# RWKV-6 attention and a tanh-shrink MLP in one kernel: unused matmuls in the boot's waits, and the result in two parts

## The chip, the cores and the metric

The kernel runs on one core of a Trainium2 chip. The metric is the device time of one execution in microseconds (us). Its engines work in parallel, each through its own instructions in order, and wait for each other by semaphores: TensorE (PE in the profile; its weight loads are PEld), VectorE (DVE), ScalarE (ACT), GpSimd (POOL) and SyncE (SP), which issues most DMA transfers.

## The reference, cut to what matters

```python
batch, n_heads, seq, head_dim = (4, 8, 768, 48)
for t in range(S):
    cur = np.einsum('bhd,bhe->bhde', u[None] * kt, vt)
    y[:, :, t] = np.einsum('bhd,bhde->bhe', rt, state + cur)
    state = wt[:, :, :, None] * state + np.einsum('bhd,bhe->bhde', kt, vt)
# y -> x: (3072, 384)
h = x @ w_in            # 384 x 2048
g = h - np.tanh(h)
return g @ w_out        # 2048 x 384, float32
```

A recurrence over 768 steps for each of 32 heads, then a two-layer MLP on the 3072 rows that come out.

## The kernel before

The sequence is cut into 8 blocks of 384 steps (4 batches, 2 halves each). Attention of a block is made in phases: "level 1" to "level 32" build the matrix of scores between time steps inside chunks of 64 by doubling (at level m the keys and receptances of blocks of m steps are multiplied, and then decayed for the next level), "turn" transposes the keys, "update" makes the chunks' states, and "result" adds what comes from the states to what comes from the scores. While the MLP of block i runs, the phases of block i+1 are threaded between its products. Only the first block has nothing to run beside: its attention is the "boot". There the four pairs of heads are worked in two halves, h1 and h2, so that engines overlap.

A level in the boot: products on TensorE into a PSUM scratch tile (2 banks of 512 columns, of which a level uses 192 in each, and level 1 uses 384), decay on VectorE, then masked copies into the scores.

```python
def scratch(ps):
    return ps.tile([P, 2, BANK], F32, name="att", tag="att")     # 4 buffers in the boot

def level(self, ps, m, p0, n, put_off=None):
    ...                                       # cut: level 32 puts its copies off
    gr = self.gram(ps, self.tiles["kq"], self.tiles["rp"], p0, n, m, L // 2)   # TensorE, 24 products
    ins = self.decay(m, p0, n)                # VectorE: kq and rp times the decay
    if 2 * m % 32 == 0:
        ...                                   # cut: level 16 copies on ScalarE, 4 copies
        return ins
    for h in range(2):
        ...
        nc.vector.copy_predicated(out=dst, mask=mask, data=src)    # reads gr
    return ins
```

The result, all pairs of a block or half of them:

```python
def result(self, ps, pairs, holes_full=False):
    yp = [scratch(ps) for e in range(2)]
    ...
                nc.tensor.matmul(yp[p % 2][e0:e0 + 64, par, n0:n0 + L],     # from the states
                                 lhsT=St[rows, p, 2 * c + par, :], rhs=rp[rows, t0:t0 + L],
                                 start=(n == 0 and c == 0), stop=False, skip_group_check=True)
    nc.tensor.drain().then_inc(fence, 1)
    fences.append(None)
    nc.tensor.wait_ge(fence, len(fences))
    ...
                nc.tensor.matmul(yp[p % 2][e0:e0 + D, par, n0:n0 + L],      # from the scores
                                 lhsT=self.v[toks, c, f0:f0 + D], rhs=A[toks, h, p, c, :],
                                 start=False, ...)
    ...                                       # ScalarE copies yp to xT; holes_full: 48 rows at a time
```

The boot and the main loop:

```python
def boot(ps, blk, later):
    h1, h2 = HALVES
    ...                                       # loads, mix
    masked = blk.level_1(ps, h1)              # products; the masked copy comes later
    blk.decay(1, h1, UP)
    blk.totals(1, h1, UP)
    blk.mix(h2, UP, copy=nc.scalar.copy)
    masked()
    blk.level(ps, 2, h1, UP)
    masked = blk.level_1(ps, h2)
    blk.decay(1, h2, UP)
    ...
    masked()
    for m in (2, 4, 8, 16, 32):
        for p0 in HALVES:
            if (m, p0) != (2, h1):
                ins = blk.level(ps, m, p0, UP, last)
            ...
    for p0 in HALVES:
        blk.turn(ps, p0)                      # transposes; ScalarE copies ks
    for copies in last:
        copies()                              # level 32's copies, ScalarE
    later.mix(0, NPAIR, ("kmix",))            # ScalarE
    for p0 in HALVES:
        blk.update(ps, p0)                    # products, then 24 VectorE instructions on the states
    blk.result(ps, [h1, h1 + 1])
    blk.fill_holes([nc.sync, nc.scalar, nc.gpsimd])
    converted()                               # weights made ready by ScalarE and VectorE
    ready.append(convert(*raws.pop(0)))
    converted()
    ins = blk.result(ps, [h2, h2 + 1], True)
    begin_behind(ins, more_weights(nc.sync))  # a weight load that starts with the result's first copy
    ...

for f in range(NF):                           # main loop, a block's 16 slices of the MLP
    g, next_rest, made = first(here, f, ps_d) # products hp, then ScalarE and VectorE
    ...
    if f in phases:
        later.phase(ps_a, phases[f])
    ...
    if len(waiting) > LAG:
        s, fs, gs = waiting.pop(0)
        s.add(fs, gs)                         # products acc of slice f - 3
```

Of the kernel before, what the change touches and what calls it, by code (L numbers as in the profile page):

```python
# [37 lines left out]
F32 = mybir.dt.float32  # L38
# [46 lines left out]
def kernel(  # L85
# [26 lines left out]
    u_sb = const.tile([P, NPAIR], F32, name="u_sb", tag="u_sb")  # L112
    nc.scalar.dma_start(out=u_sb, in_=uT)

    warm = const.tile([P, 1], F32, name="warm", tag="warm")
    nc.scalar.activation(out=warm, in_=shift[:, 0:1], func=AF.Copy)

# [57 lines left out]
            lambda: nc.vector.tensor_tensor(out=a, in0=a, in1=up, op=ALU.add)]  # L175


    def scratch(ps):
        return ps.tile([P, 2, BANK], F32, name="att", tag="att")

    fence, fences = tc.alloc_semaphore("fence"), []

    class Block:
# [189 lines left out]
                        in1=kvp[:, c % 2, n0:n0 + D], op0=ALU.mult, op1=ALU.add)  # L373
            return ins

        def result(self, ps, pairs, holes_full=False):


            St, rp = states[self.q], self.tiles["rp"]
            yp = [scratch(ps) for e in range(2)]  # L380
            slots = [pairs[n:n + 2] for n in range(0, len(pairs), 2)]
            for n, slot in enumerate(slots):
                for c in range(NCP):
                    for par in range(2):
                        for p in slot:
                            for h in range(2):
                                rows = slice(64 * h, 64 * h + D)
                                e0 = 64 * (h ^ (p % 2))
                                t0 = p * NB + (2 * c + par) * L
                                n0 = (n * NCP + c) * L  # L390
                                nc.tensor.matmul(yp[p % 2][e0:e0 + 64, par, n0:n0 + L],  # L391
                                                 lhsT=St[rows, p, 2 * c + par, :],
                                                 rhs=rp[rows, t0:t0 + L],
                                                 start=(n == 0 and c == 0), stop=False,
                                                 skip_group_check=True)

            nc.tensor.drain().then_inc(fence, 1)  # L397
            fences.append(None)
            nc.tensor.wait_ge(fence, len(fences))
            for n, slot in enumerate(slots):  # L400
                for p in slot:
                    for c in range(NCP):
                        for h in range(2):
                            for par in range(2):
                                toks = slice(64 * par, 64 * par + 64)
                                e0 = 64 * (h ^ (p % 2))
                                f0 = p * D2 + h * D
                                n0 = (n * NCP + c) * L
                                nc.tensor.matmul(yp[p % 2][e0:e0 + D, par, n0:n0 + L],  # L409
                                                 lhsT=self.v[toks, c, f0:f0 + D],  # L410
                                                 rhs=A[toks, h, p, c, :],
                                                 start=False,
                                                 stop=(n == len(slots) - 1 and c == NCP - 1),
                                                 skip_group_check=True)
            copies = []
            for n, slot in reversed(list(enumerate(slots))):
                for p in reversed(slot):
                    src = yp[p % 2][:, :, n * NCP * L:(n + 1) * NCP * L].rearrange(
                        "e a (c t) -> e c a t", t=L)
                    dst = self.xT[:, p, :] if p < KC else self.late  # L420
                    dst = dst.rearrange("e (c a t) -> e c a t", a=2, t=L)
                    for rows in (slice(0, D), slice(64, 64 + D)) if holes_full else (slice(0, P),):
                        copies.append(nc.scalar.copy(out=dst[rows], in_=src[rows]))  # L423
            return copies[0]

# [9 lines left out]
        def phase(self, ps, name):  # L435
            if name == "level 1":
                for p0 in HALVES:
                    self.level_1(ps, p0)()
            elif name == "turn":
                for p0 in HALVES:  # L440
                    self.turn(ps, p0)
            elif name == "update":
                for p0 in HALVES:
                    self.update(ps, p0)
            elif name == "result":
                self.result(ps, list(range(NPAIR)))
                self.fill_holes([nc.sync])
            else:
                self.level(ps, name, 0, NPAIR)
# [67 lines left out]

    def plan(i):

        names = ("level 1", 2, 4, 8, 16, 32, "turn", "update", "result")  # L520
# [12 lines left out]
        return dict(zip(steps, names)), before, behind, converted, loads, urgent  # L533
# [18 lines left out]
    def boot(ps, blk, later):  # L552

        h1, h2 = HALVES
        for p0 in HALVES:
            for name, src in (("kq", kT), ("rp", rT), ("wt", wT)):
                blk.load(name, src, p0, UP)
        for name in ("rmix", "kmix"):
            blk.tiles[name] = inp.tile([P, NPAIR * NB], F32, name=name, tag=name)
        more_weights(nc.sync)  # L560
        blk.load_v()
        for _ in range(2):
            more_weights(nc.sync)
        blk.mix(h1, UP, copy=nc.vector.tensor_copy)
        masked = blk.level_1(ps, h1)
        blk.decay(1, h1, UP)
        blk.totals(1, h1, UP)
        blk.mix(h2, UP, copy=nc.scalar.copy)
        masked()
        blk.level(ps, 2, h1, UP)  # L570
        masked = blk.level_1(ps, h2)
        blk.decay(1, h2, UP)
        blk.totals(1, h2, UP)
        for m in (2, 4, 8, 16):
            blk.totals(m, h1, UP)
# [64 lines left out]
    for i, blk in enumerate(blocks):  # L640
# [7 lines left out]
        for f in range(NF):  # L648
# [81 lines left out]
```

## Time and profile before

| | |
|---|---|
| median of 3 runs | 667.45 us (667.01 to 667.76) |
| span of the profiled execution | 665.8 us |
| TensorE busy | 642.6 us, 97% |
| VectorE busy | 545.2 us, 82% |
| ScalarE busy | 488.7 us, 73% |
| mean granted TensorE clock in the records | 0.990 |

The page lists for each engine how long it was busy and for groups of instructions their mean duration, and in 40 slices how busy each engine was. A slice is 16.6 us here, so the boot is the first three. The line for TensorE's granted clock shows full speed in every slice but the third, where it is 5 tenths. The trace can also be asked for the busy time in any stretch, for the instructions that write one tile (smallest, median and largest duration in ns), and for the instructions in order of time; a row of that list has start, duration, engine, line, operation, output and inputs, shape, and how many were merged, and in brackets how long the engine stood idle before and what ended it. One fp32 product shows as two TensorE passes, so 24 products are 48 passes.

The chain of waits, followed back from the last instruction, is TensorE for 80% of the span, VectorE 5%, ScalarE 4%, weight loads 4%.

### The profile page before, as it was taken

What the parts mean: (1) busy time and instruction counts of PE and PEld (TensorE: products, weight loads), DVE (VectorE), ACT (ScalarE), POOL (GpSimd) and SP (SyncE); (2) the same over time, 40 slices, a digit from 0 to 9 for tenths busy, and PEclk for the clock granted to TensorE, in tenths of its full rate; (3) what the DMA queues carried; (4) which work ended last, traced back from release to release, by engine and by line L of the source; (5) the groups of instructions that cost most, each with busy time, mean ns of one, the idle gap of its engine ahead of it and who ended that gap; (6) DMA issues with size and microseconds to landing.
All of it is one profiled execution on the core that took longest, in us unless ns stands there. A gap on an engine that the chain in (4) does not pass through costs nothing.

```text
span 665.8 us, 19964 instructions
## 1 busy us (share of the span) xinstructions
PE 642.6 (97%) x8480; PEld 412.0 (62%) x8480; DVE 545.2 (82%) x1101; ACT 488.7 (73%) x966; POOL 4.6 (1%) x19
## 2 busy tenths in 40 slices
PE   5879999999999999999999999999999999999997
PEld 4756656566665666666665666656666566655554
DVE  7789999899768997599885997689985999747664
ACT  4668998875868667785767758686677857768785
POOL 2000000000000000000000000000000000000000
PEclk9959999999999999999999999999999999999999
DMA  8656432532312122222212231123132200001000
GB/s 318 220 181 226 135 128 81 188 106 65 96 33 89 58 63 84 58 72 56 91 50 57 73 97 50 56 63 108 49 96 58 71 3 2 2 10 37 0 0 36
DMA packets 30841, 54.37 MB, mean 82 GB/s; under 512 B 2336, under 2 KB 28704, under 8 KB 30752
## 3 DMA queue, kind: packets, MB, share of 16 engines
q1 hardware_dynamic: 30336, 52.80, 24.5%
q8 instruction: 67, 1.10, 0.7%
q10 hardware_dynamic: 352, 0.25, 0.1%
q14 instruction: 22, 0.18, 0.1%
q0 software_dynamic: 64, 0.05, 0.0%
HBM read 47.19 MB, written 4.72 MB: 78 GB/s over the span
## 4 chain that ended last, share of the span: by engine, by line
PE 80%; DVE 5%; issue 4%; PEld 4%; ACT 4%; DMA 1%; PEldq 1%; SPq 0%; DVEq 0%
PE acc L509 33%; PE hp L471 32%; PE att L242 9%; PE att L409 2%; DVE states L371 2%; PEld hp L471 2%; PEld att L391 2%; PE att L342 2%; PEld acc L509 1%; PE att L319 1%; DMA wt<-in_wT 1%; DVE rp L274 1%; DVE w_sb L175 1%; ACT scores L330 1%; PEldq L397 1%
## 5 line engine op out<-in xcount | busy, mean ns | idle before, releaser
L471 PE MATMUL hp<-xT,w_sb 128*128 128x384 f32 x768 | 271.5, 490 | 3.8 <-ACT xT L423 2.1
L509 PE MATMUL acc<-w_sb,gT 128*128 128x384 f32 x768 | 273.6, 493 | 0.8 <-issue 0.8
L471 PEld LDWEIGHTS hp<-xT,w_sb 128*128 128x128 f32 x768 | 145.9, 191 | 108.0 <-ACT xT L423 2.3
L509 PEld LDWEIGHTS acc<-w_sb,gT 128*128 128x128 f32 x768 | 140.5, 190 | 89.5 <-ACT o L514 2.3
L478 ACT ACTIVATE h<-hp 128x384 f32<-128x384 f32 x128 | 62.6, 489 | 138.9 <-PE hp L471 138.1
L493 DVE TENSOR_TENSOR th<-h,th 128x384 f32<-128x384 f32 x128 | 71.0, 555 | 46.1 <-ACT th L482 46.0
L488 DVE SCALAR_TENSOR_TENSOR hs<-h,s 128x384 f32<-128x384 f32 x128 | 71.0, 555 | 26.3 <-ACT s L479 26.3
L496 DVE COPY_PREDICATED gT<-big,th 128x384 f32<-128x384 int32 x128 | 76.2, 595 | 12.8 <-ACT h L478 0.5
L480 ACT ACTIVATE qa<-s,shift 128x384 f32<-128x384 f32 x128 | 78.8, 615 | 4.2
L488 DVE SCALAR_TENSOR_TENSOR gT<-qb,hs 128x384 f32<-128x384 f32 x128 | 71.4, 558 | 9.3
L483 ACT ACTIVATE big<-s,shift 128x384 f32<-128x384 f32 x128 | 76.8, 600 | 0.0
L481 ACT ACTIVATE qb<-s,shift 128x384 f32<-128x384 f32 x128 | 76.8, 600 | 0.0
L488 DVE SCALAR_TENSOR_TENSOR hs<-qa,hs 128x384 f32<-128x384 f32 x128 | 70.6, 552 | 0.0
L479 ACT ACTIVATE s<-h 128x384 f32<-128x384 f32 x128 | 67.0, 524 | 4.0
L482 ACT ACTIVATE th<-h 128x384 f32<-128x384 f32 x128 | 64.9, 507 | 0.0
L242 PEld LDWEIGHTS att<-rp,kq 48*64 48x64 f32 x3072 | 53.4, 145 | 18.3 <-issue 12.6
L242 PE MATMUL att<-rp,kq 48*64 48x32 f32 x3072 | 57.5, 229 | 2.0 <-DVE rp L274 0.9
L274 DVE TENSOR_TENSOR kq<-kq,tot 128x768 f32<-128x768 f32 (+1 forms) x45 | 38.7, 859 | 2.9 <-PE att L242 1.5
L371 DVE SCALAR_TENSOR_TENSOR states<-states,tot,att 128x48 f32<-128x48 f32 x176 | 31.5, 259 | 9.1 <-PE att L360 9.1
L274 DVE TENSOR_TENSOR rp<-rp,tot 128x768 f32<-128x768 f32 (+1 forms) x45 | 38.8, 863 | 0.0
L302 DVE COPY_PREDICATED scores<-mask_all,att 128x384 f32<-128x384 uint8 (+1 forms) x54 | 31.9, 656 | 0.0
L242 PE MATMUL att<-rmix,kmix 48*64 48x64 f32 x768 | 15.3, 239 | 7.4 <-ACT rmix L222 7.4
(54 smaller groups left out, 339.4 us busy)
## 6 DMA issues: line engine op xcount, KB each, us to landing
raw<-in_weights SPq DMA_DIRECT2D x16, 768.0 KB, 4.9
rmix<-in_rT SPq DMA_DIRECT2D x7, 768.0 KB, 4.7
kmix<-in_kT SPq DMA_DIRECT2D x7, 768.0 KB, 4.8
wt<-in_wT SPq DMA_DIRECT2D x7, 768.0 KB, 4.8
kq<-in_kT SPq DMA_DIRECT2D x7, 768.0 KB, 5.7
rp<-in_rT SPq DMA_DIRECT2D x7, 768.0 KB, 4.6
v_sb<-in_v SPq DMA_DIRECT2D x8, 576.0 KB, 4.2
out_y<-o SPq DMA_DIRECT2D x23, 192.0 KB, 1.9
```

The costliest lines, as they stand in the source:

```text
L242: nc.tensor.matmul(dst, lhsT=lhs[rows, t0:t0 + L], rhs=src, start=True, stop=True)
L274: ins = nc.vector.tensor_tensor(out=part, in0=part, in1=by, op=ALU.mult)
L471: nc.tensor.matmul(hp, lhsT=w_in_sb[:, f, kc, :], rhs=xT[:, kc, :], start=(kc == KC - 1), stop=(kc == 0))
L479: nc.scalar.activation(out=s, in_=h, func=AF.Square)
L480: nc.scalar.activation(out=qa, in_=s, func=AF.Square, bias=shift[:, 0:1])
L481: nc.scalar.activation(out=qb, in_=s, func=AF.Square, bias=shift[:, 1:2])
L482: nc.scalar.activation(out=th, in_=h, func=AF.Tanh)
L483: nc.scalar.activation(out=big, in_=s, func=AF.Relu, bias=shift[:, 2:3])
L488: return lambda: nc.vector.scalar_tensor_tensor(out=out, in0=in0, scalar=scalar, in1=in1, op0=op0, op1=ALU.mult)
L493: lambda: nc.vector.tensor_tensor(out=th, in0=h, in1=th, op=ALU.subtract),
L496: lambda: nc.vector.copy_predicated(out=g, mask=big.bitcast(I32), data=th)], made
L509: nc.tensor.matmul(acc, lhsT=g[:, j * P:(j + 1) * P], rhs=w_out_sb[:, f, :], start=(f == 0), stop=(f == NF - 1))
```

## The change

It has three parts. (1) `result` becomes two functions, so that the products of an MLP slice stand between the products from the states and those from the scores; the wait for the fence is then meant to fall behind other work. (2) In the boot's first half, the products from the scores come first, as they are ready before the states; they leave the rows between heads untouched, so this half is copied 48 rows at a time too. (3) Unused fp32 products of a constant are put on TensorE where the boot leaves it waiting, to keep it busy[...]. They write columns of the last scratch tile that its phase doesn't use. Their results are read by nothing.

```diff
+    idle_in = const.tile([P, NB], F32, name="idle_in", tag="idle_in")
+    nc.vector.memset(idle_in, 1.0)
...
+    last_scratch = []
     def scratch(ps):
-        return ps.tile([P, 2, BANK], F32, name="att", tag="att")
+        last_scratch[:] = [ps.tile([P, 2, BANK], F32, name="att", tag="att")]
+        return last_scratch[0]
...
-        def result(self, ps, pairs, holes_full=False):
+        def from_states(self, yp, slots, first):      # the first loop of result; 48 columns wide if second
+        def from_scores(self, yp, slots, first):      # the second loop of result
+        def result_1(self, ps, pairs, part="from_states"):
+            yp = [scratch(ps) for e in range(2)]
+            slots = [pairs[n:n + 2] for n in range(0, len(pairs), 2)]
+            getattr(self, part)(yp, slots, True)
+            nc.tensor.drain().then_inc(fence, 1)
+            fences.append(None)
+            return yp, slots
+        def result_2(self, yp, slots, apart=False, part="from_scores"):
+            nc.tensor.wait_ge(fence, len(fences))
+            getattr(self, part)(yp, slots, False)
             ...                                       # the copies
...
     def boot(ps, blk, later):
         h1, h2 = HALVES
+        def keep_busy(n, width):
+            for _ in range(n):
+                nc.tensor.matmul(last_scratch[0][:, 0, BANK - width:], lhsT=idle_in[:, 0:P],
+                                 rhs=idle_in[:, 0:width], start=True, stop=True)
+        scratch(ps)
+        keep_busy(5, NB)
...
         masked = blk.level_1(ps, h1)
+        keep_busy(2, P)
...
         blk.level(ps, 2, h1, UP)
+        keep_busy(1, 320)
         masked = blk.level_1(ps, h2)
+        keep_busy(2, P)
...
                 if (m, p0) != (2, h1):
                     ins = blk.level(ps, m, p0, UP, last)
+                    keep_busy(1, 320)
...
-        blk.result(ps, [h1, h1 + 1])
+        blk.result_2(*blk.result_1(ps, [h1, h1 + 1], "from_scores"), True, "from_states")
...
-        ins = blk.result(ps, [h2, h2 + 1], True)
+        ins = blk.result_2(*blk.result_1(ps, [h2, h2 + 1]), True)
+        keep_busy(2, 320)
...
             if len(waiting) > LAG:
                 s, fs, gs = waiting.pop(0)
                 s.add(fs, gs)
+            if later and phases.get(f) == "result 1":
+                later.phase(ps_a, "result 2")
```

(Cut and condensed: the plan's names and the two loops' `start` and `stop` flags follow from this.)

More of the change, by code (lines that the diff above doesn't have):

```diff
@@ L374, in update @@
             return ins
-        def result(self, ps, pairs, holes_full=False):
-            St, rp = states[self.q], self.tiles["rp"]
-            yp = [scratch(ps) for e in range(2)]
-            slots = [pairs[n:n + 2] for n in range(0, len(pairs), 2)]
+        def from_states(self, yp, slots, first):
+            St, rp, width = states[self.q], self.tiles["rp"], L if first else D
             for n, slot in enumerate(slots):
@@ L390, in result @@
                                 n0 = (n * NCP + c) * L
-                                nc.tensor.matmul(yp[p % 2][e0:e0 + 64, par, n0:n0 + L],
-                                                 lhsT=St[rows, p, 2 * c + par, :],
+                                nc.tensor.matmul(yp[p % 2][e0:e0 + width, par, n0:n0 + L],
+                                                 lhsT=St[rows, p, 2 * c + par, 0:width],
                                                  rhs=rp[rows, t0:t0 + L],
-                                                 start=(n == 0 and c == 0), stop=False,
+                                                 start=(first and n == 0 and c == 0),
+                                                 stop=(not first and (n, c) == (len(slots) - 1, NCP - 1)),
                                                  skip_group_check=True)
-            nc.tensor.drain().then_inc(fence, 1)
-            fences.append(None)
-            nc.tensor.wait_ge(fence, len(fences))
+        def from_scores(self, yp, slots, first):
             for n, slot in enumerate(slots):
@@ L411, in result @@
                                                  rhs=A[toks, h, p, c, :],
-                                                 start=False,
-                                                 stop=(n == len(slots) - 1 and c == NCP - 1),
+                                                 start=(first and n == 0 and c == 0),
+                                                 stop=(not first and (n, c) == (len(slots) - 1, NCP - 1)),
                                                  skip_group_check=True)
+        def result_1(self, ps, pairs, part="from_states"):
[8 more added lines that the diff above has]
+            getattr(self, part)(yp, slots, False)
             copies = []
@@ L421, in result @@
                     dst = dst.rearrange("e (c a t) -> e c a t", a=2, t=L)
-                    for rows in (slice(0, D), slice(64, 64 + D)) if holes_full else (slice(0, P),):
+                    for rows in (slice(0, D), slice(64, 64 + D)) if apart else (slice(0, P),):
                         copies.append(nc.scalar.copy(out=dst[rows], in_=src[rows]))
@@ L444, in phase @@
                     self.update(ps, p0)
-            elif name == "result":
-                self.result(ps, list(range(NPAIR)))
+            elif name == "result 1":
+                self.parts = self.result_1(ps, list(range(NPAIR)))
+            elif name == "result 2":
+                self.result_2(*self.parts)
                 self.fill_holes([nc.sync])
@@ L518, in plan @@
     def plan(i):
-        names = ("level 1", 2, 4, 8, 16, 32, "turn", "update", "result")
+        names = ("level 1", 2, 4, 8, 16, 32, "turn", "update", "result 1")
         if i == 0:
```

## The prediction

> **What bounds the kernel now.** I read the page's 40 slices first: TensorE is at 9 tenths in every slice but the first three, so from about 50 us on the matmuls set the time (547.11 of the 550 us from 110 to 660 are TensorE busy in the table by stretches), and only the boot, roughly 0 to 50 us, has waits to fill. Then the table of stretches, for the granted clock:
>
> ```profile
> 32.07:35.48 3.41, 1.39 (x67) 1.11 (x60) 3.41 (x21) 2.55 (x8) 0.00 (x0) 1.00 0.65 253
> 35.48:49.13 13.65, 10.98 (x217) 7.92 (x221) 10.79 (x19) 9.13 (x15) 1.11 (x2) 0.50 0.54 176
> ```
>
> The columns are TensorE, weight load, VectorE, ScalarE, GpSimd busy, the clock, DMA. A stretch of 3.41 us in which TensorE worked 1.39 us is followed by 13.65 us at half clock. Next the instructions that write the boot's scratch tile, in the boot and in the steady part:
>
> ```profile
> L242 PE MATMUL att<-rp,kq x384: 207/291/313, 8.0 to 24.8; 48*64 48x32 f32 x192
> L342 PE MATMUL att<-ident,kq x12: 417/417/473, 27.0 to 29.4; 128*128 128x128 f32 x12
> ...
> L242 PE MATMUL att<-rp,kq x2592: 219/219/240, 62.2 to 556.5; 48*64 48x32 f32 x200
> L342 PE MATMUL att<-ident,kq x84: 272/273/273, 88.7 to 566.8; 128*128 128x128 f32 x84
> ```
>
> The same passes take 291 ns before 25 us and 219 after 62, the transposes 417 against 273. So the boot is slow from its start to 32 us too, although the clock column says 1.00 there: it has no record before 32.07 and counts that as full. The boot is at half clock for all but 3.4 of its 49 us. Last, the order of time on VectorE and TensorE:
>
> ```profile
> 18.23 0.55 DVE L274 TENSOR_TENSOR kq<-kq,tot 128x384 f32<-128x384 f32 x1
> 18.70 0.55 DVE L274 TENSOR_TENSOR rp<-rp,tot 128x384 f32<-128x384 f32 x1
> 19.17 0.62 DVE L302 COPY_PREDICATED scores<-mask_all,att 128x192 f32<-128x192 uint8 x2
> ...
> 17.93 6.02 PE L242 MATMUL att<-rp,kq 48*64 48x32 f32 x187 [0.54 <-DVE rp L274]
> 26.99 2.82 PE L342 MATMUL att<-ident,kq 128*128 128x128 f32 x12
> 29.74 2.65 PE L360 MATMUL att<-v_sb,ks 64*64 64x48 f32 x96
> 43.31 4.21 PE L471 MATMUL hp<-xT,w_sb 128*128 128x384 f32 x6 [2.07 <-ACT xT L423]
> ```
>
> A half-level (one level of one half) costs VectorE two decays and two mask copies, 18.23 to 19.70, or 1.47 us. Its 48 passes cost the cold TensorE about 1.5 us (6.02 us for 187 is 32 ns each). The two engines run beside each other here: while VectorE works on one half, TensorE makes the products of the other.
>
> **What the Trainium skill says.** "TensorE: Matmul & The Clock Gate", section "Part 1: The HAM clock gate", says that half rate is the default, that a busy window of about 3.4 us opens the clock and an idle one closes it. The trace agrees: 13.65 us is four windows of 3.41, and the stretch with 1.39 us of work closed it. The section puts no number on how busy the window must be; in this trace 2.41 us of work at 42.31 to 45.72 did not open it and 3.41 us at 45.72 to 49.13 did. The same part's trace caveats call the clock records unreliable, which fits the missing record before 32 us. Its section "Part 3: Packing small matmuls — row/col tiling" says that matmuls start and end in strict program order. That is what decides this case: a matmul that waits holds up all those behind it.
>
> **The change, part by part.**
>
> First, the opening five unused products: ten passes of 384 columns, at the cold spacing of the first dense product (4.21 us for six; 0.64 us between starts) at most 6.4 us, from about 1.65 (after the new constant is written, a quarter of the 1.34 us that VectorE takes for the four times larger scores memset) to 8.1 at the latest. They fill a window, so the clock should open between 5 and 8.5 us. The real products began at 6.33; they now begin at 7 to 8 but run faster. VectorE's first level-2 decay stood at 9.60; I put it at about 10.0.
>
> Second, and this is the core, the unused 320-column product behind each half-level. In the built program, listed engine by engine with what each instruction waits for, it waits for that half-level's own mask copies on VectorE (at level 16 for ScalarE's copies), although it writes other columns of the tile. The dependency is taken for the tile. So TensorE stands until the copies end, then runs the unused product, then the products of the other half, and only then can VectorE begin on that half. What ran side by side becomes a chain. One link, cold: 0.14 to wake TensorE (17.79 to 17.93 in the trace) + two passes of 0.64 x 320/384 = 0.53, so 1.07 + 48 passes 1.51 + 0.12 to wake VectorE + 1.47 of VectorE = 4.3 us. Warm: 0.14 + 0.54 + 0.80 (half of a steady 1.60 us for 96 passes) + 0.12 + 1.47 = 3.1 us. Before, 1.47.
>
> Which clock? After level 2 of the second half TensorE has nothing between about 14.6 and 17.2 us, as VectorE does decays, totals and masks, so some window there holds at most some 40% of work, as little as the one that closed the clock before. Afterwards a cold link has (1.07 + 1.51) / 4.3 = 60% work, less than the 71% (2.41 of 3.41) that did not open it. So I take cold as the main case.
>
> Running it forward, cold: level 2 of the second half ends at about 17.2 (was 16.46). Four links for levels 4 and 8: 34.4 (was 22.80). Level 16 twice, 2.84 of TensorE and waking + 1.26 of ScalarE's copies: 42.6 (was 26.4). The two last levels, 0.76 us each, with an unused product before and after: 47.5. Transposes 2.8: 50.3, where they ended at 29.81. That is +20.5. Warm: 29.6, 35.6, 38.4, and with transposes of 1.4, 39.8: +10.
>
> Third, the result of the first half from scores first. The old order stood waiting for the states. The new one has its scores 2.57 us after the second ks copy (eight ScalarE copies), then about 2.7 us for the rest of the products, the fence and the products from states (cold). Then ScalarE alone: four copies instead of two 1.94, two DMA issues 1.50, one conversion 1.73, and the second half's copies begin 10.5 us after the ks copy; they did at 41.32 - 30.65 = 10.67. So -0.2 cold, some -1.3 warm. The two unused products behind it start after half of these copies and may hold the first dense product up by a microsecond, but the ScalarE conversion behind its 4.7 us weight load releases that stage anyway (h begins at 47.79, the product ended at 47.52). I count +0.5.
>
> Fourth, the split result in the seven later blocks: between its two kinds of products TensorE pauses from 189.42 (last start) to 189.75, 0.33 us, most of it a drain that stays. At best 0.15 x 7 = 1 us; I count -0.5.
>
> Sum, cold: 20.5 - 0.2 + 0.5 - 0.5 = +20.3, or about 688; warm: 10 - 1.3 + 0.3 - 0.5 = +8.5, or 676. After the boot all blocks run in their old order on a full TensorE, so what the boot loses nothing gives back. In the cold case TensorE is busy without pause from 42.6 to 50.3, which probably opens the clock before the transposes, so -1.5. I predict 685 us.
>
> **The rivals.** (a) The unused products work as meant: the clock stays open and the waits cost little. For it: half clock costs the boot in the transposes (1.4 us), the L360 passes, both results, the first dense product (2.1 us) and the last levels, and halved they would give some 5 us: 662. Against it: the wait on the copies, which is in the program. (b) The chain is there, but the clock stays open: 676. For it: the unused products were sized for that. Against it: a warm link has only 1.34 / 3.1 = 43% work, and the stretch of 1.39 in 3.41, 41%, closed the clock. (c) The clock swings between both: 678 to 684. (d) Cold throughout: 688.
>
> **Range and chances.** I give (a) 5%, (b) 20%, (c) 25%, (d), with or without an opening at its end, 50%. That puts the middle near 685 with 674 to 690 holding eight in ten. 2% is 13.3 us, so slower means above 680.8: most of (d) and half of (c), and some room for links longer than I made them, 0.68. Within 2%: 0.29. Faster, below 654.1, would need more than all that half clock costs: 0.03.
>
> **What would show it.** In the time order of the changed boot, each 320-column product should begin just after a mask copy ends, and VectorE's decay just after a group of products ends, with VectorE idle about 2.8 us (cold) or 1.6 us (warm) at each link; the transposes end near 50 us (40 warm) and the first dense product starts 18 to 20 us (8 to 10 warm) later than 43.31. The duration of the 48x32 products tells the clock: 291 cold, 219 warm. If VectorE shows no such idle time, the wait costs nothing and I am wrong by the whole sum; if the links stand at 3.1 us I am wrong by the clock only. The steady blocks should not differ by more than 1 us in sum.

## The result, and the profile after

The changed kernel takes 686.57 us (median of 4 runs, 686.29 to 687.09) against 667.23 (666.73 to 667.76) measured beside it: 1.0291 times as long, 95% interval 1.0273 to 1.0308. The profiled span grew from 665.8 to 684.7 us. The page of the changed kernel, part 2 and two groups of part 5 (busy us and mean ns, then the idle time before the group and what ended most of it):

```profile
PE   7677999999999999999999999999999999999998
...
PEclk9556999999999999999999999999999999999999
...
L279 DVE TENSOR_TENSOR kq<-kq,tot 128x768 f32<-128x768 f32 (+1 forms) x45 | 38.7, 860 | 23.0 <-PE att L247 18.2
...
L578 PE MATMUL att<-idle_in 128*128 128x320 f32 (+2 forms) x42 | 24.4, 713 | 16.4 <-DVE scores L307 11.0
```

A slice is 17.1 us now and the first four are below 9 tenths for TensorE, where there were three of 16.6 (the last slice is below in both kernels). The unused products (L578) waited 11.0 us for VectorE's mask copies, and the decays on VectorE (L279) waited 18.2 us for products: two waits that feed each other. The clock is low in the second to fourth slice. By stretches (columns as before: TensorE, weight load, VectorE, ScalarE, GpSimd, clock, DMA share, GB/s):

```profile
7.61:14.44 6.83, 4.65 (x155) 3.53 (x154) 4.99 (x12) 4.16 (x8) 0.00 (x0) 1.00 1.04 409
14.44:51.99 37.55, 25.96 (x461) 17.25 (x460) 14.34 (x37) 7.37 (x16) 0.00 (x0) 0.50 0.25 84
51.99:58.81 6.82, 4.50 (x204) 3.71 (x202) 4.76 (x25) 6.39 (x17) 0.26 (x1) 1.00 0.58 221
58.81:69.05 10.24, 8.92 (x102) 5.70 (x102) 9.21 (x16) 7.93 (x12) 0.86 (x2) 0.50 0.59 203
```

The opening products did open the clock, for 6.83 us. Then it was at half for 37.55 us, in which TensorE was "busy" 69% and VectorE 38%. The order of time on TensorE, start and duration first:

```profile
12.51 0.81 PE L578 MATMUL att<-idle_in 128*128 128x320 f32 x2 [2.18 <-DVE scores L307]
...
18.56 1.44 PE L578 MATMUL att<-idle_in 128*128 128x320 f32 x2 [2.07 <-DVE scores L307]
19.93 1.51 PE L247 MATMUL att<-rp,kq 48*64 48x32 f32 x48
23.12 1.43 PE L578 MATMUL att<-idle_in 128*128 128x320 f32 x2 [1.68 <-DVE scores L307]
24.48 1.51 PE L247 MATMUL att<-rp,kq 48*64 48x32 f32 x48
...
50.64 2.14 PE L347 MATMUL att<-ident,kq 128*128 128x128 f32 x12
...
65.71 3.83 PE L489 MATMUL hp<-xT,w_sb 128*128 128x384 f32 x6
```

and on VectorE in the same stretch:

```profile
21.50 0.56 DVE L279 TENSOR_TENSOR kq<-kq,tot 128x384 f32<-128x384 f32 x1 [2.81 <-PE att L247]
21.98 0.55 DVE L279 TENSOR_TENSOR rp<-rp,tot 128x384 f32<-128x384 f32 x1
22.45 0.62 DVE L307 COPY_PREDICATED scores<-mask_all,att 128x192 f32<-128x192 uint8 x2
26.05 0.56 DVE L279 TENSOR_TENSOR kq<-kq,tot 128x384 f32<-128x384 f32 x1 [2.99 <-PE att L247]
```

Read them together as one ring. VectorE's copies end at 23.07 (22.45 + 0.62), the unused product starts at 23.12, the other half's products at 24.48, and VectorE's next decay at 26.05, after 2.99 us idle. One link, decay to decay, is 4.55 us; before it was 1.47. The boot's transposes begin at 50.64 instead of 26.99, and the first dense product at 65.71 instead of 43.31.

Where the 18.8 us of span (684.65 less 665.85) came from, each as the difference of two starts or ends in the two traces:

| stretch | before | after | difference |
|---|---|---|---|
| start to the end of the transposes | 29.81 | 52.78 | +22.97 |
| from there to the second half's first result copy | 11.51 | 9.30 | -2.21 |
| from there to the first dense product | 1.99 | 3.63 | +1.64 |
| first block of the main loop | 79.48 | 77.24 | -2.24 |
| the six after it | 471.82 | 470.49 | -1.33 |
| the last | 71.23 | 71.23 | 0 |

### The profile page after: what moved, and what is told of

It reads as the page before. It is cut to its first block, busy times and chain, and to the rows that moved or that the text cites. A ratio compares the mean times of both kernels' runs of the same rounds, so it can differ in the third digit from the quotient of the medians.

```text
span 684.7 us, 20048 instructions
## 1 busy us (share of the span) xinstructions
PE 660.1 (96%) x8522; PEld 416.1 (61%) x8522; DVE 546.1 (80%) x1102; ACT 489.8 (72%) x968; POOL 4.6 (1%) x19
## 4 chain that ended last, share of the span: by engine, by line
PE 90%; ACT 6%; DVE 2%; issue 1%; PEld 0%; PEldq 0%; DVEq 0%; ACTq 0%
PE acc L527 35%; PE hp L489 35%; PE att L247 9%; PE att L578 4%; PE att L411 2%; PE att L393 2%; PE att L365 1%; PE att L347 1%; PE att L324 1%; ACT w_sb L172 1%; ACT up L174 1%; DVE scores L307 1%; ACT scores L300 1%; ACT s L497 1%; ACT scores L335 1%
## 5 line engine op out<-in xcount | busy, mean ns | idle before, releaser
L279 DVE TENSOR_TENSOR kq<-kq,tot 128x768 f32<-128x768 f32 (+1 forms) x45 | 38.7, 860 | 23.0 <-PE att L247 18.2
L578 PE MATMUL att<-idle_in 128*128 128x320 f32 (+2 forms) x42 | 24.4, 713 | 16.4 <-DVE scores L307 11.0
L279 DVE TENSOR_TENSOR rp<-rp,tot 128x768 f32<-128x768 f32 (+1 forms) x45 | 38.8, 863 | 0.0
```

The lines of the kernel that those rows point to most:

```text
L279: ins = nc.vector.tensor_tensor(out=part, in0=part, in1=by, op=ALU.mult)
```

## The experiments

My theory: the loss is the wait of the unused product for the copies of its own half-level, and the half clock that goes with the chain. Rivals: it is the unused products' own time on TensorE; or it is the other two parts of the change. All ratios are to the kernel before, with 95% intervals; each kernel starts from the changed one.

**1. Without the unused products.**

```diff
-        scratch(ps)
-        keep_busy(5, NB)
...                          # and all other keep_busy calls; the rest of the change stays
```

> The changed kernel without any unused product: the result in two parts and the scores first in h1, nothing else. My theory (the unused product behind each half-level waits for that half-level's copies and makes a chain of TensorE and VectorE): the 19 us come from the unused products alone, so this stands within 1.5 us of the kernel before, 666 to 668 us, transposes ending near 29.8 us as before. Rival (the split result costs time, through its later copies or a changed order in the seven later blocks): 672 us or more.

Measured: 666.18 us, 0.9985 (0.9975 to 0.9996). The whole loss, and a little more, belongs to the unused products.

**2. Narrow ones: same places, same waits, 16 columns instead of 320.**

```diff
-                    keep_busy(1, 320)
+                    keep_busy(1, 16)
```

> The unused product behind each level is 16 columns wide instead of 320, at the same place, so the wait stays and most of its work goes. My theory: nine of them lie on the chain at about 1.37 us each, of which some 0.25 stays for one; 676 us, with VectorE's pauses at each link near 1.8 us instead of 2.9. Rival (the width, that is the work, is what costs): 667 to 669 us. Rival (the wait alone costs, the work lies beside): 686 us.

Measured: 678.62 us, 1.0158 (1.0142 to 1.0173). TensorE's order of time in this kernel:

```profile
17.71 0.61 PE L578 MATMUL att<-idle_in 128*128 128x16 f32 x2 [2.07 <-DVE scores L307]
18.25 1.51 PE L247 MATMUL att<-rp,kq 48*64 48x32 f32 x48
21.44 0.61 PE L578 MATMUL att<-idle_in 128*128 128x16 f32 x2 [1.68 <-DVE scores L307]
```

A link is 3.73 us, 0.82 less, and that is the product: it holds the queue for 0.54 us (17.71 to 18.25) instead of 1.37. Nine such products account for 7.4 of the 8.0 us between this kernel and the changed one. The other 11 us over the kernel before stay although a link's unused product is now short. The rival that it is the products' own time explains some 8 us of 19 and no more. The run is 2.6 us slower than expected: 0.54 us of each product stayed, not 0.25.

**3. The same product ahead of the copies.** The product is put between the half-level's products and its copies, so that nothing it depends on is still running.

```diff
                 gr = self.gram(...)
                 ins = self.decay(m, p0, n)
+                put_off[0]()                 # keep_busy(1, 320), ahead of the copies
                 ...                          # the copies
-                    keep_busy(1, 320)        # after level()
```

> The unused product of each half-level is put between that half-level's products and its copies, so that it waits for nothing; the same number and width of unused products as in the changed kernel. My theory: without the wait VectorE's links go back to about 1.5 us; if the clock stays open 660 to 664 us, if it closes at level 2 and opens again 664 to 672 us; in any case at least 14 us under the changed kernel. Rival (the unused products cost the time by the time they take on TensorE, wherever they stand): about 686 us.

Measured: 665.58 us, 0.9963 (0.995 to 0.9976). TensorE and then VectorE in this kernel:

```profile
17.48 0.81 PE L582 MATMUL att<-idle_in 128*128 128x320 f32 x2
18.43 0.90 PE L247 MATMUL att<-rp,kq 48*64 48x32 f32 x48
19.26 0.81 PE L582 MATMUL att<-idle_in 128*128 128x320 f32 x2
...
28.98 0.28 PE L328 MATMUL att<-rp,kq 48*32 48x32 f32 x10 [2.30 <-issue]
```

```profile
18.20 0.63 DVE L311 COPY_PREDICATED scores<-mask_all,att 128x192 f32<-128x192 uint8 x2
18.73 0.56 DVE L279 TENSOR_TENSOR kq<-kq,tot 128x384 f32<-128x384 f32 x1
19.20 0.55 DVE L279 TENSOR_TENSOR rp<-rp,tot 128x384 f32<-128x384 f32 x1
19.66 0.63 DVE L311 COPY_PREDICATED scores<-mask_all,att 128x192 f32<-128x192 uint8 x2
```

The same number of unused products of the same size, and no bracket (no idle time to speak of) on either engine in this stretch: VectorE goes from copies to decay without a pause, 1.46 us from 18.20 to 19.66, as before the change. The clock is open from 6.78 to 37.49 us. So the order of one product against two copies is worth 21 us. This also shows what the open clock is worth: it makes 48 passes take 0.90 us instead of 1.51, but VectorE needs 1.47 for its half-level anyway, so the levels gain nothing from it. And TensorE stalled 2.30 us until 28.98 with no wait that the profile shows ("issue", below), and the transposes end at 31.30 us, later than the 29.81 of before. With the clock open 660 to 664 us had been expected.

**4. No unused products at the levels; the opening ones, those of level 1 and the end pair stay.**

```diff
-                    keep_busy(1, 320)        # and the one behind level 2 of the first half
```

> The changed kernel without the unused product behind each level; the five at the start, those behind level 1 and the two at the end stay. My theory: the chain is gone, the clock opens near 7.6 us and closes by 15 us, so little is won by it: 666 to 669 us. Rival (an early open clock carries on through the boot by itself): 660 to 663 us.

Measured: 665.85 us, 0.997 (0.996 to 0.998). The clock opens at 4.88 and closes at 11.70, and the boot runs at half clock until 32.18, like before. It is as fast as the version with the clock open through the boot (experiment 3). What the products at the levels buy is within the intervals. So the half clock by itself costs next to nothing here: it costs where it makes the links of a chain longer.

**5. The unused products into a PSUM tile of their own,** behind the copies as in the change. A tile of two banks had to go: the scratch has three buffers instead of four.

```diff
-                nc.tensor.matmul(last_scratch[0][:, 0, BANK - width:], lhsT=idle_in[:, 0:P],
+                nc.tensor.matmul(own[:, BANK - width:], lhsT=idle_in[:, 0:P],
...
-        scratch(ps)
+        own = ps.tile([P, BANK], F32, name="own", tag="own", bufs=1)
...
-    with tc.tile_pool(name="ps_boot", bufs=4, space=PSUM) as ps_boot:
+    with tc.tile_pool(name="ps_boot", bufs=3, space=PSUM) as ps_boot:
```

> The unused products stay where the changed kernel has them, behind the copies in program order, with number and width unchanged, but write a PSUM tile of their own; the scratch tile gets three buffers instead of four to make room. My theory (they wait because they share the tile that the copies read): no wait is left, VectorE's links are about 1.5 us again, 664 to 667 us, like the kernel with the early unused products. Rival (their place in the order makes the chain, not the tile): 684 us or more. Rival (three buffers are too few): between 668 and 680 us, with products waiting for older copies.

Measured: 670.46 us, 1.0043 (1.0018 to 1.0068); TensorE in this kernel:

```profile
19.40 0.90 PE L247 MATMUL att<-rp,kq 48*64 48x32 f32 x48
20.23 0.81 PE L578 MATMUL own<-idle_in 128*128 128x320 f32 x2
...
28.37 0.28 PE L324 MATMUL att<-rp,kq 48*32 48x32 f32 x10 [2.40 <-issue]
...
31.68 1.54 PE L347 MATMUL att<-ident,kq 128*128 128x128 f32 x6 [0.89 <-ACT ks L349]
34.11 2.81 PE L365 MATMUL att<-v_sb,ks 64*64 64x48 f32 x96 [0.89 <-ACT ks L349]
```

The same program order, another tile, and the wait is gone: level 8 of the second half ends at 22.46 us, in the changed kernel at 36.6. So the wait was for the tile and not for any data; the columns were different ones all along. It is still some 5 us slower than experiment 3. Two things differ in the traces: the second transposes and the updates wait 0.89 us each for ScalarE's copies (with four buffers only the updates do, 0.23 us), and the clock closed at 29.13 us instead of 37.49, so that the updates took 2.81 us instead of 1.62. How the 5 us divide was not tried.

**6. The pair at the end of the boot.** Experiment 3 without it, and then with it on a scratch tile that is free:

```diff
-        keep_busy(2, 320)                    # early_no_end
+        scratch(ps)                          # early_free_end: this ahead of the pair instead
```

> The early unused products, without the two at the end of the boot. In the run with them the first dense product began 2.1 us after it could have (44.16 against 42.5, the end of the second half's copies, is 1.7 us) and ended at 48.1, later than the weight conversion at 47.1 that ScalarE has before h. My theory: the dense product begins 1.6 us earlier, still at half clock, h begins about 1 us earlier, 664.5 us. Rival (the two at the end open the clock earlier and are worth it): 666 us or more.

Measured: 665.77 us, 0.996 (0.9946 to 0.9974), the same as with the pair; the microsecond that was expected did not come. (The expectation's 2.1 us is 44.16 less 42.5, or 1.7.)

> The early unused products, with the two at the end written to a scratch tile that is free by then, so that they don't wait for the result's copies and run while ScalarE copies. My theory: the first dense product begins as soon as its input is copied, 1 us earlier than in the early run, and the clock may open one window (3.4 us) sooner; 664 to 665 us. Rival (the end is set by the weight load that starts with the copies, so nothing moves): 665.6 us.

Measured: 666.99 us, 0.9996 (0.9971 to 1.002), and not one kind of execution: eight of twelve took 664.34 to 667.71 us at a mean clock of 0.994 to 1.000, four took 670.95 to 671.39 at 0.98. The profiled one is of the four. Its clock closed at 15.27 us although no unused product waits for a copy; just before, until 14.87, TensorE had stalled for 0.85 us (0.30 us at the same place in experiment 3, whose program is the same up to there). After that:

```profile
15.80 1.43 PE L582 MATMUL att<-idle_in 128*128 128x320 f32 x2
17.16 1.51 PE L247 MATMUL att<-rp,kq 48*64 48x32 f32 x48
18.60 1.43 PE L582 MATMUL att<-idle_in 128*128 128x320 f32 x2
...
20.07 0.63 DVE L311 COPY_PREDICATED scores<-mask_all,att 128x192 f32<-128x192 uint8 x2 [0.31 <-PE att L582]
```

With the clock at half, TensorE has more to do per half-level (15.80 to 18.60, 2.80 us) than VectorE (1.47). The real products stand behind the unused ones, and VectorE's copies now wait for the unused product (0.31 us), as both use the same tile. So the no-wait version has a fragile side: it pays only while the clock stays open.

**7. A product in both places,** ahead of the copies and behind them: an attempt to keep the clock open while the wait stays.

```diff
-        blk.level(ps, 2, h1, UP)
+        blk.level(ps, 2, h1, UP, [lambda: keep_busy(1, 320)])   # and keep_busy(1, 320) behind it stays
```

> Two unused products for each half-level: one in front of the copies, which waits for nothing, and one behind them, which waits as in the changed kernel. It has the changed kernel's chain with more work on TensorE, to keep the clock open. If the clock stays open, a link is about 3.2 us instead of 4.55, seven of them and the last levels give some 12 us back: 674 to 677 us. That is the cost of the waits at full clock. Rival (the clock is a consequence and counts for little): 684 us or more. If the clock closes all the same: 686 us or more, and this tells nothing on it.

Measured: 691.47 us, 1.0355 (1.033 to 1.038). The clock closed at 14.13 all the same, so this says nothing of an open clock; it only added another cold product to each link (4.95 us, 23.93 to 28.88). Inconclusive for its question.

**8. The same question with stronger means:** two or three products on a tile of their own ahead of the one that waits, three scratch buffers as in experiment 5.

```diff
-                    keep_busy(1, 320)
+                    keep_busy(3 if m == 2 else 2, 320)     # own tile, waits for nothing
+                    wait_behind()                          # 320 columns of the scratch, waits for the copies
```

> The changed kernel's chain with the clock kept open: behind each half-level's copies the unused product that waits for them as in the changed kernel, and in front of it two or three more in a PSUM tile of their own that wait for nothing and fill the time in which VectorE works. Only the links are read from it (three scratch buffers change the boot's end). Rival b of the prediction, the chain at full clock: a link of 3.1 to 3.3 us instead of 4.55. If the links stay at 4.3 us or more with passes of 219 ns, the clock isn't what makes a link longer than my warm sum.

Measured: 680.56 us (one run, no interval), clock open from 6.44 to 57.64. Its chain:

```profile
20.41 0.81 PE L582 MATMUL att<-idle_in 128*128 128x320 f32 x2 [0.41 <-DVE scores L307]
21.15 0.90 PE L247 MATMUL att<-rp,kq 48*64 48x32 f32 x48
21.98 1.34 PE L578 MATMUL own<-idle_in 128*128 128x320 f32 x4
23.73 0.81 PE L582 MATMUL att<-idle_in 128*128 128x320 f32 x2 [0.41 <-DVE scores L307]
```

A link is 3.32 us with the clock open and 4.55 with it closed; 1.47 without the wait. The transposes begin at 41.81, against 50.64 in the changed kernel and 26.99 before. So of the 23.7 us that the change adds by then, 14.8 are there at full clock and 8.8 go with the half clock. This division is rough: the kernel also has two or three more products per half-level, which stand on the chain from level 16 on, and three buffers.

**9. The other two parts alone.** The split result in the later blocks only, and the scores-first order in the boot only; both without unused products.

```diff
-        blk.result_2(*blk.result_1(ps, [h1, h1 + 1], "from_scores"), True, "from_states")
+        blk.result_2(*blk.result_1(ps, [h1, h1 + 1]))                  # split_only
...
-                self.parts = self.result_1(ps, list(range(NPAIR)))
+                self.result_2(*self.result_1(ps, list(range(NPAIR))))  # boot_only
```

> The kernel before with the result in two parts in the seven later blocks alone; the boot is as before. In the changed kernel's trace a later block takes 78.41 us and every one the same; before, five take 78.22 and two 79.47, where a result's products stand still for 1.2 us in the middle of a group without a semaphore. My theory: the split costs 0.2 us a block and takes those stalls away, as a slice's three long products between the two groups leave time for whatever the short ones outrun (TensorE's instructions, by the queue of instruction packets): about 666 us, 1 to 1.5 us under the kernel before, every later block at 78.41. Rival (the gain of the two parts lies in the boot): no difference to the kernel before.

Measured: 666.79 us, 0.998 (0.9972 to 0.9989).

> The kernel before with the scores first in the boot's first half alone; the later blocks' results are in one piece. My theory: the boot's end is set by ScalarE (four copies instead of two, two DMA issues, a conversion), so nothing comes of it: within 0.7 us of the kernel before, and the stalls of 1.2 us in later blocks are there again. Rival (the scores first save the wait for the states): 1 us or more faster.

Measured: 668.55 us, 1.0005 (0.9992 to 1.0018). Scores-first is worth nothing that can be measured; the split is worth 0.2%. Why can be read in one result of a later block, first in the kernel before (the view begins within the first group, which has 96 passes):

```profile
344.79 1.29 PE L391 MATMUL att<-rp,states 48*64 48x64 f32 x76
346.19 1.22 PE L409 MATMUL att<-scores,v_sb 64*48 64x64 f32 x72
348.44 0.55 PE L409 MATMUL att<-scores,v_sb 64*48 64x64 f32 x24 [1.03 <-issue]
348.93 2.20 PE L509 MATMUL acc<-w_sb,gT 128*128 128x384 f32 x6
```

and with the split alone:

```profile
345.05 1.63 PE L391 MATMUL att<-rp,states 48*64 48x64 f32 x96
346.79 2.20 PE L525 MATMUL acc<-w_sb,gT 128*128 128x384 f32 x6
348.92 1.56 PE L409 MATMUL att<-scores,v_sb 64*48 64x64 f32 x96
```

In the first, TensorE stops in the middle of the products from the scores for 1.03 us, with "issue" as the cause: it waits for nothing that the profile shows. Of the seven full-length blocks of the kernel before, four (not five) last 78.22 us; two last 79.47, and these have such a stop (ending at 348.44 and 584.37); the first, at 79.48, has one that ends at 108.77. With the split every block but the first and last lasts 78.41 us and none has one. So the split costs 0.19 us per block and takes two stops of 1.25 us away. The order alone (boot_only) has both stops back.

**10. The parts that were worth something:** experiment 3 without the end pair, the old order in the boot, and two unused products at level 2.

```diff
-        blk.level(ps, 2, h1, UP)
-        keep_busy(1, 320)
+        blk.level(ps, 2, h1, UP, [lambda: keep_busy(2, 320)])
```

> The no-wait version with what the other runs showed to be worth nothing taken back: no pair at the end of the boot, the first half's products from the states first as before, two unused products per half-level at level 2 instead of one, the result still in two parts in the later blocks. The theory of the waits (an unused product placed ahead of the copies waits for nothing) expects VectorE's links to stay at 1.47 us and the clock to stay open through level 2 and on to some 35 us: 664 to 666 us. The rival (the clock doesn't depend on those products any more, or the additional ones only take TensorE's time) expects no better than the 665.8 us of the version with one product each and no pair at the end; a clock that closes early all the same would show as some runs near 670.

Measured: 665.87 us, 0.9971 (0.9962 to 0.998). The clock was open from 4.65 to 28.54, so the added products did not hold it to 35 us, and a stall (1.50 us, until 27.56) came in level 32 as in experiment 3. It is no better than experiments 3 and 4 and experiment 6 without the pair. These four stand 0.3 to 0.4% below the kernel before. The split alone gives 0.2% and both other parts 0.15% (experiments 9 and 1), so at most some 0.2% is left for unused products that cause no wait.

## Why the prediction was right

Predicted 685.0, measured 686.57 us. By its steps:

- **The opening products** were to end by 8.1 us and open the clock between 5 and 8.5. They ended at 8.00 (1.49 + 6.51), and the clock opened at 7.61. VectorE's first level-2 decay came at 10.53 (predicted 10.0). Right.
- **The wait for the tile, and so the chain.** Right in kind, and shown from both sides: another tile (own_tile) or another place (early) and the chain is gone. The trace agrees with the Trainium skill, "TensorE: Matmul & The Clock Gate", section "Part 3: Packing small matmuls — row/col tiling": matmuls go in strict program order, here seen as 2.07 us in which the other half's 48 products, whose inputs had been ready since 11.5 us, stood behind one that was of no use.
- **The link,** 4.3 us predicted, 4.55 measured. From one start to the next: VectorE and waking TensorE 1.62 (predicted 0.14 + 1.47), products and waking VectorE 1.57 (1.51 + 0.12), unused product 1.36 (1.07). Only the last term was mis-sized: I had counted its two passes at the spacing of a stream, 0.53 each, but they started 0.69 us apart and the next products 0.67 later; why was not tried. VectorE's idle time at a link, 2.8 us predicted, was 2.81 to 3.00.
- **The whole chain** ended 2.5 us later than summed (52.78, not 50.3). It began 1.1 us late: level 2 of the second half ended at 18.30, not 17.2, after VectorE had waited 0.29 us for level 1's unused products and 0.46 us for the products behind them, which I had not counted. What followed, with nine unused products, took 2.0 us more than summed, and the transposes 0.66 less.
- **The clock.** Half clock during levels 4 to 32 was the main case, and the passes show it; the instructions on the scratch tile in the changed kernel, between 14 and 52 us:

```profile
L247 PE MATMUL att<-rp,kq x336: 291/291/313, 15.0 to 43.6; 48*64 48x32 f32 x168
```

  291 ns, not 219. The clock that the opening products had opened closed at 14.44, before the first whole link, after a window with 57% of work. The idle 1.48 us of that window belong to a wait that I had not summed, that of the first 320-column product for its copies (2.18 us, until 12.51). I had the clock close later, in the idle time from 14.6 to 17.2, after a window with 40%: right outcome, wrong window.
- **The first half's result and the clock's second opening.** I took 1.5 us off for a clock that opens before the transposes and 0.2 for scores-first. The clock opened during the transposes (51.99), and these took 2.14 instead of 2.82 us; from the end of the ks copies to the second half's copies it was 8.42 us (53.66 to 62.08), not 10.5. The products took 1.66 after the last score copy, at open clock (I had 2.7, cold), and the two DMA issues of 0.61 and 0.84 ran beside ScalarE's copies, where I had added 1.50 in series. In the table this stretch is -2.21, against -1.7 predicted.
- **The pair behind the boot** was +0.5; the stretch to the first dense product grew by 1.64. But the block behind it is shorter by 2.24:

```profile
43.31:122.79 79.48, 76.83 (x1034) 47.57 (x1035) 74.30 (x145) 72.71 (x132) 0.00 (x0) 0.96 0.52 176
```

```profile
65.71:142.95 77.24, 75.56 (x1035) 46.71 (x1035) 74.15 (x145) 71.23 (x131) 0.00 (x0) 0.98 0.53 175
```

  This is the first block before, then after: 1.27 us less TensorE time for the same passes, as fewer of them fall at half clock, and 0.97 us less idle, most of it the stop of 0.81 us that ended at 108.77 before. Early_no_end shows the pair's net effect as none. I had said that what the boot loses nothing gives back: the first dense product came 22.4 us later (18 to 20 predicted), and 3.6 of these were given back behind it.
- **The split** was -0.5 us, for a fence that gets out of the way. The size was nearly right for a wrong reason: it costs 0.19 us a block, and takes away stops that I had not seen in the trace, -1.33 us in six blocks. I had said that steady blocks would not differ by more than 1 us in sum.
- **The sum.** The working comes to 688 - 1.5 = 686.5 us, or 18.8 more in span; I gave 685, the middle with the rivals' chances. The span did grow by 18.8, but its terms were off by +2.5 (chain), -0.5 (first half's result), +1.1 (pair), -2.2 (first block) and -0.8 (the six after it). That these cancel is luck. The wait and the chain, which make the sign and most of the size, are not.
- **A reading.** The last of the 40 slices before stands at 7 tenths, not 9. It bears on nothing: the last block takes 71.23 us in both kernels.
- **The rivals.** (a), a clean open clock at 662 us, was too good even for the versions that had it: 665.6 in experiment 3, and 665.93 in the one execution of early_free_end with a mean recorded clock of 1.000. The levels go at VectorE's pace, and TensorE then stalls by itself. (b), the chain at open clock, 676: the run built for it took 680.6, with a link of 3.32 us (3.1 predicted) and three buffers, at which it has the waits of 0.89 us of own_tile too; how the 4.6 us over 676 divide was not tried.

What stays open: what decides whether the clock closes or opens after a window, and the cause of the "issue" stalls, for which only an inference is given below.

## What to carry to other kernels

Filler work for an idle engine must wait for nothing: ask of each filler instruction which tile it touches and who still reads that tile, because the wait that the program gets is for the tile, not for the columns, and everything behind it in the queue waits too. Placed ahead of that reader, it must be done in time, or the reader waits for it. Then ask what an open clock is worth where the idle is: if another engine sets the pace there (here VectorE, 1.47 us per half-level against 0.90 or 1.51 on TensorE), it is worth next to nothing. When a link of a chain is summed, take a product behind a wait at its own measured cost and not at the spacing within a stream.

## What the runs showed of the hardware

**The clock gate has no simple threshold of busy time.** The Trainium skill's "TensorE: Matmul & The Clock Gate", section "Part 1: The HAM clock gate", names a busy window of about 3.4 us to open and an idle one to close. The stretches here are indeed multiples of 3.41 us. But the windows that ended in a closing were far from idle. For the changed kernel, no_level and early_free_end, the last window before the clock closed:

```profile
11.03:14.44 3.41, 1.93 (x53) 1.43 (x54) 3.34 (x10) 1.72 (x2) 0.00 (x0) 1.00 1.05 411
```

```profile
8.29:11.70 3.41, 2.07 (x100) 1.89 (x92) 3.41 (x8) 2.34 (x6) 0.00 (x0) 1.00 1.06 412
```

```profile
11.86:15.27 3.41, 2.28 (x86) 1.73 (x86) 3.31 (x9) 1.50 (x2) 0.00 (x0) 1.00 1.04 416
```

TensorE was busy 57%, 61% and 67% of the time in these. In early it stayed open after one with 50%:

```profile
27.26:30.68 3.42, 1.70 (x20) 1.46 (x21) 1.11 (x3) 0.00 (x0) 0.00 (x0) 1.00 0.57 208
```

And a half clock can stay with TensorE never idle, as in early_free_end, over five windows:

```profile
15.27:32.34 17.07, 17.07 (x329) 11.43 (x322) 10.42 (x28) 7.30 (x16) 0.00 (x0) 0.50 0.36 115
```

So busy time in the trace doesn't decide it alone. One weighting sorts the windows better: count each pass as its columns times the share of the 128x128 array that its weights fill, rows and columns rounded up to 32 (a 48x64 pass fills a quarter, an unused product all of it), and lay it back from its recorded end at the 0.83 or 1.67 ns a column that 384 columns take in a stream (0.32 us at full, 0.64 at half clock). In the first 75 us of all fourteen traces, 19 windows at half clock opened it, each with 1496 columns or more, and 66 did not, each with 1472 or fewer; the five above have 1191 to 1392 each, and the next, which opened it, 1648. For closing, a line at 1490 sorts all but 5 of 160 windows. The weighting was chosen after the fact and no run was made to test it.

**TensorE stalls by itself in runs of short products.** The stops with "issue" in the kernel before come at passes 222, 475, 729, 1868, 5044 and 8221: 253, 254, 1139, 3176 and 3177 apart, which is 2, 2, 9, 25 and 25 times 127 within 4. A pass is a weight load and a matmul, so 127 passes are 254 instructions. Part 3 of the page has a queue for instructions:

```profile
q8 instruction: 67, 1.10, 0.7%
```

2 x 8480 instructions of TensorE divided by 67 packets is 253, and in the trace each of these six stops ends 1.3 to 1.5 us after such a packet has landed (1.2 to 1.5 us for those of early and own_tile). It fits that TensorE, at some 17 to 32 ns per pass, uses up its instructions faster than they come, and that slow products between the short ones (the split) let the fetch catch up. This is an inference from positions and times; nothing was run that changes the fetch. It cost up to 2.4 us at one place (own_tile), as much as the half clock did in the transposes and updates (2.82 + 2.65 us before, 1.47 + 1.62 in early).
